# A fused attention and state-space kernel: small VectorE work moved to GpSimd, table chains reordered, 86 quads in place of 84

## The chip, the core and the metric

The kernel runs on one core of a Trainium2 chip. The metric is the device time of one execution in microseconds (us); less is better. The core has five engines with a queue each: TensorE (PE, matrix products; its weight loads are listed as PEld), ScalarE (ACT), VectorE (DVE), GpSimd (POOL) and SyncE (SP), which issues nearly all DMAs.

## The reference

The input is one sequence of 2048 positions and 512 features. Cut to what matters:

```python
g = sigmoid((x * gate_w).sum(-1, keepdims=True))
# A: softmax attention, 32 heads of 16
q, k, v = split(x @ wqkv)
p = softmax(einsum("bhqd,bhkd->bhqk", q, k) * 16 ** -0.5)
a = merge(einsum("bhqk,bhkd->bhqd", p, v)) @ wo
# B: a state-space convolution over the sequence, per feature d
P = exp(dt * A[:, :, None] * l)             # complex, l = 0 .. 2047
K = einsum("dn,dnl,dn->dl", C, P, dt * B).real
b = causal_conv(x, K) + x * Dskip           # by FFT in the reference
out = g * a + (1 - g) * b
```

## The kernel before

**Attention.** The 32 heads by 2048 keys by 2048 queries are cut into tiles of 128 keys by 512 queries. Four tiles (four heads, one key block) make a q step; there are 512 q steps in 32 blocks of 16, 2048 tiles in all. Tiles are put into 683 groups of three. For a group g, `qk` computes the score tiles into one of two PSUM buffers (SC0, SC1), and `ex` takes the exponential of the group in one ScalarE instruction (line 939) into a ring of tiles ET/EX. `pv` multiplies a finished q step with the values VE into the PSUM bank OA; one column of VE is 1, so that the sum of the softmax comes along. After 16 q steps `norm_a` transposes OA into OT (line 994); for each pair of blocks `norm_b` takes the reciprocal (L1000), a gate factor in the later half (L1003), and the product ON (L1006); `norm_c` transposes ON into OnT (L1011).

**Quads.** To spare ScalarE, some q steps are done by VectorE: `decide` inserts the four tiles of such a step, one per group, as third tiles of four groups, and ScalarE then runs over two tiles only. VectorE evicts each of the four score tiles with one multiply-add into 16-bit integers, which read as bf16 are a rough exponential (`bits`, tile DZ, L960). `batch` adds three constants (CUTS) to the whole quad, giving three more versions, DU (L974, 2048 integers per partition each), and `sums` adds all four versions up through value products on TensorE. `win` decides whether a quad may start: it needs a window of groups (WIN, from group 190 to 674), a distance from the last quad, and a count of quads under a line with slope 1 per RATE groups; `decide` also wants idle VectorE time in the plan.

**State-space part.** `params` builds powers of the complex decay (L1 to L80, M1 to M9) by squaring and complex products on VectorE, `powers`, `weights` and `zpart` build the tables B16 and Z for each quarter of the features (`tables` for the first, `bases` for the others, which go through DRAM), and for each of 16 blocks of features a table T is multiplied out. `kstage` makes the taps with matrix products into the PSUM bank MB, transposes them into Kt (L1311), and copies rows of them with shifts into Ks (L1315 and L1318), which goes to DRAM (gm_kd). From there come the Toeplitz tiles H, and `ystage` computes the convolution with the rows U (from `xrows`) into MB, gated into Yst (L1406).

**Order.** The program is not written out by hand: generators (`norms`, `projs`, `tables` and the others) yield pieces of work with an engine, a cost and a priority, and a planner (`Sched.fill`) puts them between the groups by its own model of each engine's time, in which each operation has a cost `c`. The queues are then fixed, in the planned order, with semaphore waits; `place` gives the tiles their SBUF addresses. The function `zero` issues products with a zero tile wm between the useful ones, with amounts FILL. Paced DMAs wait for a marker (`tk`) that the exponential of an earlier group sets.

Of the kernel before, what the change touches and what calls it, by code (L numbers as in the profile page):

```python
# [39 lines left out]
SPLAG = .8  # L40
PTM = 3.2
# [11 lines left out]
RATE = 5.9  # L53
RATE2 = 5.4
# [72 lines left out]
class Prog:  # L127
# [68 lines left out]
    def ready(self, a):  # L196
        eng, R, W = a[1][0], a[1][2], a[1][3]
        lag = SPLAG if a[0] == self.dma else .05
        t = 0.0
        for acc, wr in ((R, False), (W, True)):  # L200
            for b, sl, *tag in acc:
                st = b.st.get(sl)
                if not wr and (st is None or not st[0] or (tag and b.tags.get(sl) != tag[0])):
                    return None
                if st is None:
                    continue
                for d in (st[0], st[1]) if wr else (st[0],):
                    for s, i in d.items():
                        if s != "PE" or eng != "PE":
                            t = max(t, self.fin[(s, i)] + (.03 if s == eng else self.marg.get((s, i), DMARG) if isinstance(s, tuple) else DLAG if eng == 'PE' and s == 'DVE' else lag))  # L210
        return t
# [65 lines left out]
    def dma(self, eng, fn, R=(), W=(), c=.45, lat=3.0, m=DMARG, pace=False, b=.1):  # L277
# [12 lines left out]
        at = self.tm[eng]  # L290
        for s2, k2 in deps.items():
            at = max(at, self.fin[(s2, k2)] + (.08 if isinstance(s2, tuple) else SPLAG))
# [195 lines left out]
def declare(nc, es):  # L488
# [56 lines left out]
    for n in ("WW", "WN", "L1", "L2", "L4", "L8", "L16", "L32", "L64", "L80", "M1", "M2", "M4", "M8", "M9", "pt1", "pt2"):  # L545
        sb(n, 2 * D, FP32)
# [120 lines left out]
def dap(t, off, dims):  # L667
    return bass.AP(tensor=t, offset=off, ap=[list(d) for d in dims])

# [5 lines left out]
def record(nc, p, B, ins):  # L675
# [290 lines left out]
    def batch(i):  # L966
# [5 lines left out]
        for n, (u, cut) in enumerate(zip(us, CUTS)):  # L972
            yield ("DVE", .6)
            op("DVE", lambda v, u=u, cut=cut: v.tensor_scalar(u.u16(0, [[1, 2048]]), z.u16(0, [[1, 2048]]), float(cut), None, ALU.add),  # L974
               R, [(u, 0, i)], c=.07 + 2048 / 3840)
            sch.mark(f"u{i}.{n}")
# [19 lines left out]
    def norm_b(b, n):  # L996
        w = b % 2 + 1 - n
        R = [(OT, x, b - b % 2 + x) for x in range(w, w + n)]
        K = range(w, w + n)
        op("DVE", lambda v: v.reciprocal(Rz(16 * w, [[16, n], [1, 16]]), OT(512 * w + 16, [[512, n], [32, 16]])), R, [(Rz, x) for x in K], c=.22 + .02 * n)  # L1000
        qc = b // 8
        if qc >= 2:
            op("DVE", lambda v: v.tensor_tensor(Rz(16 * w, [[16, n], [4, 4], [1, 4]]), Rz(16 * w, [[16, n], [4, 4], [1, 4]]),  # L1003
                                                B["gq"](4 * (qc - 2), [[0, n], [1, 4], [8, 4]]), ALU.mult),
               [(Rz, x) for x in K] + [(B["gq"], j) for j in range(4)], [(Rz, x) for x in K], c=.12)
        op("DVE", lambda v: v.tensor_tensor(ON(16 * w, [[16, n], [32, 16], [1, 16]]), OT(512 * w, [[512, n], [32, 16], [1, 16]]),  # L1006
                                            Rz(16 * w, [[16, n], [1, 16], [0, 16]]), ALU.mult), R + [(Rz, x) for x in K], [(ON, x) for x in K], c=.07 + .27 * n)

# [19 lines left out]
    def cmul(o, x, y, kind=""):  # L1028

        o, x, y, t1, t2 = B[o], B[x], B[y], B["pt1"], B["pt2"]  # L1030
# [13 lines left out]
    def square(o, x, conj=False):  # L1044
# [5 lines left out]
        tt("DVE", half(o, 0), half(t1, 0), half(t1, 1), ALU.subtract, [(t1, 0)], [(o, 0)], F5)  # L1050
        yield ("DVE", F5)
        op("DVE", lambda v: v.scalar_tensor_tensor(o(D, [[1, D]]), x(0, [[1, D]]), -2.0 if conj else 2.0, x(D, [[1, D]]), ALU.mult, ALU.mult),
           [(x, 0)], [(o, 0)], c=F5)

# [14 lines left out]
    def params():  # L1069
# [7 lines left out]
        for o, x in (("L2", "L1"), ("L4", "L2"), ("L8", "L4")):  # L1077
            yield from square(o, x)
        sch.mark("L8")
        for o, x in (("L16", "L8"), ("L32", "L16"), ("L64", "L32")):  # L1080
            yield from square(o, x)
        yield from square("M1", "L64", True)
# [3 lines left out]
        for o, a, b_, f in seq:  # L1086
# [6 lines left out]
            else:  # L1093
                tt("DVE", full(o), full(a), full(b_), f, key(a, b_), key(o), F5)
        yield from cmul("WN", "WW", "M1")
        for o, x in (("M2", "M1"), ("M4", "M2")):
            yield from square(o, x)
        sch.mark("M4")
        yield from square("M8", "M4")
        yield from cmul("M9", "M8", "L32", "xc")  # L1100
        yield from short("M8", "")
        yield from short("L32", "c")
        yield from short("M9", "")
        yield from cmul("L80", "L64", "L16")
        for n in ("L16", "L64", "L80"):
            yield from short(n, "n")

    def weights(qr, last, top):

        FP, t1, t2 = B["FP"], B["ft1"], B["ft2"]  # L1110
        d0 = 128 * qr
        e8 = 128 * 8
        for l, n in enumerate(("WW", "WN")):
            yield ("DVE", .38)
            op("DVE", lambda v, l=l, n=n: v.tensor_copy(FP(128 * l, [[e8, 2], [1, 128]]), B[n](d0, [[D, 2], [1, 128]])), key(n), [(FP, 0)], c=.25)
        for m, ln in ((2, "M2"), (4, "M4")):
            L, ts = B[ln], 128 * m
            yield ("LOCK", "FT")
            for ti, ri in ((t1, 0), (t2, 1)):
                yield ("DVE", dv(2 * ts))  # L1120
                tt("DVE", lambda ti=ti, ts=ts, m=m: ti(0, [[ts, 2], [128, m], [1, 128]]), lambda m=m: FP(0, [[e8, 2], [128, m], [1, 128]]),
                   lambda ri=ri, m=m, L=L: L(ri * D + d0, [[0, 2], [0, m], [1, 128]]), ALU.mult,
                   [(FP, 0), (L, 0)], [(ti, 0)], dv(2 * ts))
            for part, f in ((0, ALU.subtract), (1, ALU.add)):
                yield ("DVE", dv(ts))
                tt("DVE", lambda part=part, m=m, ts=ts: FP(part * e8 + 128 * m, [[1, ts]]), lambda part=part, ts=ts: t1(part * ts, [[1, ts]]),
                   lambda part=part, ts=ts: t2((1 - part) * ts, [[1, ts]]), f, [(t1, 0), (t2, 0)], [(FP, 0)], dv(ts))
            sch.unlock("FT")
        yield ("DVE", 1.2)
        op("DVE", lambda v: v.tensor_copy(last(0, [[last.free // 2, 2], [1, 1024]]), FP(0, [[e8, 2], [1, 1024]])), [(FP, 0)], top, c=1.2)  # L1130

    def powers(qr, last, top, *tag):

        FP, t1, t2 = B["FP"], B["ft1"], B["ft2"]
        d0, e8, l8 = 128 * qr, 128 * 8, last.free // 2

        def row(k, n=1, step=1):
            return lambda: FP(128 * k, [[e8, 2], [128 * step, n], [1, 128]])

        def rows(part, k, n=1, step=1):  # L1140
            return FP(part * e8 + 128 * k, [[128 * step, n], [1, 128]])
# [4 lines left out]
        def times(k, n, step, ln, out, W, chop=False):  # L1146
            L, ts = B[ln], 128 * n
            yield ("LOCK", "FT")
            for ti, ri in ((t1, 0), (t2, 1)):
                yield ("DVE", dv(2 * ts))  # L1150
                tt("DVE", lambda ti=ti: ti(0, [[ts, 2], [128, n], [1, 128]]), row(k, n, step),
                   lambda ri=ri: L(ri * D + d0, [[0, 2], [0, n], [1, 128]]), ALU.mult, [(FP, 0), (L, 0)], [(ti, 0)], dv(2 * ts))
            pat = [[128, n], [32, 4], [1, 32]] if chop else [[128, n], [1, 128]]
            for part, f in ((0, ALU.subtract), (1, ALU.add)):
                yield ("DVE", dv(ts))
                tt("DVE", lambda part=part: out(part), lambda part=part: t1(part * ts, pat), lambda part=part: t2((1 - part) * ts, pat), f,
                   [(t1, 0), (t2, 0)], W, dv(ts))
            sch.unlock("FT")

        def squares(k, n, out, W, chop=False):  # L1160
            ts = 128 * n
            one = [[32, 4], [1, 32]] if chop else [[1, 128]]
            pat = [[128, n]] + one
            yield ("LOCK", "FT")
            yield ("DVE", dv(2 * ts))
            tt("DVE", lambda: t1(0, [[ts, 2], [128, n], [1, 128]]), row(k, n), row(k, n), ALU.mult, [(FP, 0)], [(t1, 0)], dv(2 * ts))
            yield ("DVE", dv(ts))
            for j in range(n):
                op("DVE", lambda v, j=j: v.scalar_tensor_tensor(out(1, j, 1), FP(128 * (k + j), one), 2.0, FP(e8 + 128 * (k + j), one), ALU.mult, ALU.mult),
                   [(FP, 0)], W, c=dv(128))  # L1170
            yield ("DVE", dv(ts))
            tt("DVE", lambda: out(0), lambda: t1(0, pat if n > 1 else one), lambda: t1(ts, pat if n > 1 else one), ALU.subtract, [(t1, 0)], W, dv(ts))
            sch.unlock("FT")

        yield ("DVE", .2)
        op("DVE", lambda v: v.memset(FP(0, [[1, 128]]), 1.0), [], [(FP, 0)], c=.1)
        op("DVE", lambda v: v.memset(FP(e8, [[1, 128]]), 0.0), [], [(FP, 0)], c=.1)
        for k, n in ((1, "L1"), (2, "L2"), (4, "L4")):
            yield ("DVE", .25)
            op("DVE", lambda v, k=k, n=n: v.tensor_copy(FP(128 * k, [[e8, 2], [1, 128]]), B[n](d0, [[D, 2], [1, 128]])), key(n), [(FP, 0)], c=.22)  # L1180
        yield from times(1, 1, 1, "L2", lambda part: rows(part, 3), [(FP, 0)])
        yield from times(1, 2, 2, "L4", lambda part: rows(part, 5, 2, 2), [(FP, 0)])
        yield from squares(3, 1, lambda part, j=0, n=1: FP(part * e8 + 768, [[1, 128]]), [(FP, 0)])
# [586 lines left out]
```

## Time and profile before

| | |
|---|---|
| median of 3 runs | 801.1 us (800.99 to 801.3) |
| profiled execution | 801.08 us, span 799.3 us |
| busy in the span | PE 697.3, ACT 783.4, DVE 732.7, POOL 10.2 us |
| granted TensorE clock | 0.999 of full speed |
| DMA | 95.37 MB, mean 119 GB/s |

Times in rows of the profile are us from the start of the span, and durations in us unless called ns. A row of a group reads: line, engine, operation, output <- input, shapes, count | busy us, mean ns | idle time of the engine ahead of these instructions, and who ended it. In a row of the timeline or of the chain the first two numbers are start and length; square brackets hold idle time before it. In the stage rows the first range is the stretch, then its length, then the busy time (and instructions) of PE, PEld, DVE, ACT and POOL, the granted clock, the DMA share and GB/s. Rows of the same engine overlap at their edges: an instruction's record begins before the one ahead of it has drained.

### The profile page before, as it was taken

The numbers are of one execution on the slowest core, as the hardware profiler recorded it, in microseconds if no ns is written. First come the engines' busy times: TensorE is split into PE (matmuls) and PEld (weight loads), VectorE is DVE, ScalarE is ACT, GpSimd is POOL, SyncE is SP. The second block draws the span as 40 slices with busy tenths as digits, with TensorE's granted clock in tenths as the row PEclk, the third lists the DMA queues.
The fourth block names the chain that finished last, engine by engine and source line by source line (L and its number), as shares of the span: only waits on it lengthen the run. The fifth ranks groups of instructions, "written<-read, shape, count | busy, mean of one in ns | idle before, by whom it ended". The sixth has DMA issues, their size and how long they took to land.

```text
span 799.3 us, 29251 instructions
## 1 busy us (share of the span) xinstructions
PE 697.3 (87%) x13073; PEld 289.6 (36%) x13073; DVE 732.7 (92%) x1249; ACT 783.4 (98%) x694; POOL 10.2 (1%) x16
## 2 busy tenths in 40 slices
PE   7888888887787888989999888999989999889996
PEld 3222333432244333444434343334434444322221
DVE  7999998999999899999998999989998979899993
ACT  7999999999999999999999999999999999999995
POOL 5000000000000000000000000000000000000000
PEclk9999999999999999999999999999999999999999
DMA  9443001134365666634544555555564556531100
GB/s 211 94 89 79 9 9 37 36 103 142 111 184 149 195 168 167 177 102 132 147 106 140 173 159 161 159 132 141 144 163 121 163 149 162 134 85 53 37 22 28
DMA packets 138640, 95.37 MB, mean 119 GB/s; under 512 B 86033, under 2 KB 117138, under 8 KB 138130
## 3 DMA queue, kind: packets, MB, share of 16 engines
q1 hardware_dynamic: 136498, 92.32, 43.4%
q8 instruction: 102, 1.67, 0.9%
q10 hardware_dynamic: 2016, 1.18, 0.6%
q14 instruction: 24, 0.20, 0.1%
HBM read 65.38 MB, written 19.42 MB: 106 GB/s over the span
## 4 chain that ended last, share of the span: by engine, by line
ACT 94%; PE 3%; DVE 1%; DMA 1%; issue 0%; ACTq 0%; DVEq 0%
ACT ET L939 78%; ACT EX L939 16%; PE SC L690 1%; DMA Wk<-in_A_wqkv_dram 1%; PE MB L690 1%; PE OA L690 0%; DVE DZ L960 0%; ACTq L694 0%; DVE OT L994 0%; DVE B16s L1130 0%; DVEq L652 0%; DVE KT L780 0%; DVE ON L1006 0%; ACT ea L1073 0%; DVE fo L1731 0%
## 5 line engine op out<-in xcount | busy, mean ns | idle before, releaser
L939 ACT ACTIVATE ET<-SC 128x1536 bf16<-128x1536 f32 (+1 forms) x555 | 656.8, 1535 | 2.9 <-PE OA L690 1.7
L690 PE MATMUL SC<-Qm,KT 32*128 32x512 bf16 x2048 | 273.7, 384 | 84.3 <-ACT ET L939 65.1
L960 DVE TENSOR_SCALAR DZ<-SC 128x512 uint16<-128x512 f32 x336 | 224.1, 682 | 21.2 <-PE SC L690 19.8
L690 PEld LDWEIGHTS SC<-Qm,KT 32*128 32x128 bf16 x2048 | 70.3, 91 | 287.8 <-ACT ET L939 213.1
L974 DVE TENSOR_SCALAR DU<-DZ 128x2048 uint16<-128x2048 uint16 x252 | 165.1, 686 | 0.7
L690 PE MATMUL OA<-wm 128*32 128x256 bf16 (+3 forms) x962 | 163.5, 341 | 1.2 <-DVE wm L743 1.2
L690 PE MATMUL OA<-ET,VE 128*32 128x512 bf16 x1420 | 153.3, 389 | 1.2 <-DVE OT L994 0.9
L939 ACT ACTIVATE EX<-SC 128x1024 bf16<-128x1024 f32 (+1 forms) x128 | 147.1, 1350 | 0.0
L690 PE MATMUL OA<-DU,VE 128*32 128x512 bf16 x1008 | 96.2, 385 | 0.0
L690 PEld LDWEIGHTS MB<-U,H 128*32 128x32 bf16 x4096 | 82.0, 144 | 25.8 <-issue 16.4
L690 PE MATMUL MB<-U,H 128*32 128x128 bf16 (+7 forms) x4096 | 88.7, 225 | 1.2 <-issue 1.0
L690 PEld LDWEIGHTS OA<-ET,VE 128*32 128x32 bf16 x1420 | 39.4, 94 | 70.1 <-issue 65.6
L1015 DVE TENSOR_TENSOR T<-B,DT 128x1536 bf16<-128x1536 bf16 x64 | 59.0, 946 | 0.0
L690 PEld LDWEIGHTS OA<-wm 128*32 128x32 bf16 (+2 forms) x962 | 43.4, 94 | 16.3 <-issue 13.5
L690 PEld LDWEIGHTS MB<-T,Z 128*32 128x32 bf16 x2048 | 43.7, 155 | 10.5 <-issue 6.5
L690 PE MATMUL MB<-T,Z 128*32 128x64 bf16 (+1 forms) x2048 | 45.7, 235 | 0.2 <-issue 0.2
L690 PE MATMUL OA<-EX,VE 128*32 128x512 bf16 x292 | 40.4, 387 | 0.3 <-ACT ET L939 0.3
L690 PEld LDWEIGHTS OA<-DU,VE 128*32 128x32 bf16 x1008 | 25.7, 96 | 30.7 <-issue 21.1
L690 PE MATMUL OA<-DZ,VE 128*32 128x512 bf16 x336 | 33.0, 383 | 0.0
L994 DVE STREAM_TRANSPOSE OT<-OA 128x512 f32<-128x512 f32 x32 | 22.9, 715 | 8.9 <-PE OA L690 8.7
L1406 DVE TENSOR_TENSOR Yst<-MB,gt 128x512 bf16<-128x512 f32 x32 | 21.9, 684 | 2.0 <-PE MB L690 2.0
L1015 DVE TENSOR_TENSOR ft<-Z,DM 128x1024 bf16<-128x1024 bf16 x32 | 20.9, 686 | 0.3
(144 smaller groups left out, 445.1 us busy)
## 6 DMA issues: line engine op xcount, KB each, us to landing
H<-gm_kd SPq DMA_DIRECT2D x128, 256.0 KB, 3.6
U<-gm_xs SPq DMA_DIRECT2D x128, 134.2 KB, 2.7
T<-B SPq DMA_DIRECT2D x16, 256.0 KB, 2.6
gm_yd<-Yst SPq DMA_DIRECT2D x64, 64.0 KB, 2.7
gm_bd<-B16s SPq DMA_DIRECT2D x3, 1024.0 KB, 5.6
B<-gm_bd SPq DMA_DIRECT2D x12, 256.0 KB, 3.1
gm_kd<-Ks SPq DMA_DIRECT2D x64, 40.0 KB, 2.1
gm_xs<-xP SPq DMA_DIRECT2D x16, 136.0 KB, 2.5
```

Source lines behind the costliest of these rows:

```text
L690: op("PE", lambda t: t.matmul(out(), lhsT(), rhs(), start=start, stop=stop, skip_group_check=True, **kw), R, W, c=c, lat=.15, a=a, cfg=cfg)
L939: op("ACT", lambda a: a.activation(E(at, [[1, 512 * n]]), sc(0, [[1, 512 * n]]), AF.Exp, scale=DH ** -0.5), [(sc, i, g) for i in range(n)] ...
L960: op("DVE", lambda v: v.tensor_scalar(z.u16(512 * k, [[1, 512]]), sc(1024, [[1, 512]]), XS, XB, ALU.mult, ALU.add), [(sc, 2, g)], [(z, k, ...
L974: op("DVE", lambda v, u=u, cut=cut: v.tensor_scalar(u.u16(0, [[1, 2048]]), z.u16(0, [[1, 2048]]), float(cut), None, ALU.add), R, [(u, 0, i ...
L994: op("DVE", lambda v: v.transpose(OT(512 * w, [[1, 512]]), OA(0, [[1, 512]])), [(OA, 0, b)], [(OT, w, b)], c=.64)
L1015: op(eng, lambda v: v.tensor_tensor(o(), a(), b_(), f), R, W, c=c)
L1406: op("DVE", lambda v, w=w, h=h: v.tensor_tensor(Yst(1024 * w + 4 * h, [[128, R8], [8, 16], [1, 4]]), MB(0, [[1, R8], [R8, 16], [NC, 4]]), ...
```

## The change

- GpSimd gets the tap row copies into Ks (`kstage`), the first of the three additions of every sixth quad (numbers 3, 9, 15 and so on), one in four of the paired norm products (`norm_b` with b = 3, 11, 19, 27), and the fills of xP and gt.
- Quads may come closer (RATE 5.3 in place of 5.9 and 5.4) but only while enough tap blocks are done (`done`), which gives 86 of them by the words of the change.
- `params` is split into two threads; in it, in `weights`, `powers` and `zpart` the operations are reordered so that an operation and the one that reads its result are separated by another, with finer keys for the halves of the scratch tiles and a third scratch tile pt3. `weights` writes its last half directly into its target.
- The planner's lag for the marker of paced DMAs is 0.15 in place of 0.8 us.

```diff
+TLAG = .15
-RATE = 5.9
+RATE = 5.3
+KA = 6.5
+PKS = "POOL"
+PGS, PGR, PGN, PGM = 6, 3, 4, 1
+KB = 46
-RATE2 = 5.4
+RATE2 = 5.3
...
-                            t = max(t, self.fin[(s, i)] + (.03 if s == eng else ...
+                            t = max(t, self.fin[(s, i)] + (TLAG if b.name == "tk" else .03 if s == eng else ...
...
+def pl(n):
+    return .3 + n / 600
...
+    def done():
+        return next((k for k in range(NBLK) if f"K{k}" not in sch.flag), 99)
+
     def win(x):
         return next((w for w, (lo, hi, _, gap, *_) in enumerate(WIN) if lo <= x < hi and x >= plan["x"] + gap
-                     and len(sets) <= (min(x, XR) - WIN[0][0]) / RATE + max(x - XR, 0) / RATE2), None)
+                     and len(sets) <= (min(x, XR) - WIN[0][0]) / RATE + max(x - XR, 0) / RATE2 and done() >= KA + (x - WIN[0][0]) / KB), None)
...
         for n, (u, cut) in enumerate(zip(us, CUTS)):
-            yield ("DVE", .6)
-            op("DVE", lambda v, u=u, cut=cut: v.tensor_scalar(u.u16(0, [[1, 2048]]), z.u16(0, [[1, 2048]]), float(cut), None, ALU.add),
-               R, [(u, 0, i)], c=.07 + 2048 / 3840)
+            eng = "POOL" if n == 0 and i % PGS == PGR else "DVE"
+            yield (eng, .6)
+            op(eng, lambda v, u=u, cut=cut: v.tensor_scalar(u.u16(0, [[1, 2048]]), z.u16(0, [[1, 2048]]), float(cut), None, ALU.add),
+               R, [(u, 0, i)], c=pl(2048) if eng == "POOL" else .07 + 2048 / 3840)
...
-        op("DVE", lambda v: v.tensor_tensor(ON(...), OT(...), Rz(...), ALU.mult), ..., c=.07 + .27 * n)
+        eng = "POOL" if n == 2 and b // 2 % PGN == PGM else "DVE"
+        yield (eng, .6, 1)
+        op(eng, lambda v: v.tensor_tensor(ON(...), OT(...), Rz(...), ALU.mult), ..., c=pl(256 * n) if eng == "POOL" else .07 + .27 * n)
...
+        yield from square("M1", "L64", True)
+        sch.mark("M1")
+        for o, x in (("M2", "M1"), ("M4", "M2"), ("M8", "M4")):
+            yield from square(o, x)
+            sch.mark(o)
+
+    def params2():
+        yield ("AFTER", "L2")
...
     def zpart(qr):
...
-                for ti, xr, yr in ((t1, 0, part), (t2, 1, 1 - part)):
...
+        yield from mul(0, 0)
+        yield from mul(0, 1)
+        for u in range(1, 6):
+            yield from mul(u, 0)
+            yield from add(u - 1)
+            yield from mul(u, 1)
+        yield from add(5)
...
-        yield ("DVE", .65)
+        yield (PKS, .65)
         for q in range(2):
-            op("DVE", lambda v, q=q: v.tensor_copy(Ks(5 * HW * q + HW, ...
+            op(PKS, lambda v, q=q: v.tensor_copy(Ks(5 * HW * q + HW, ...
...
-            op("DVE", lambda v, k=k: v.memset(xP(k * T * XW, [[XW, T], [1, 16]]), 0.0), [], [(xP, (0, k))], c=.45)
+            op("POOL", lambda v, k=k: v.memset(xP(k * T * XW, [[XW, T], [1, 16]]), 0.0), [], [(xP, (0, k))], c=.45)
...
-        op("DVE", lambda v: v.memset(B["gt"](0, [[1, NC]]), 0.0), [], [(B["gt"], j) for j in range(8)], c=.2)
+        op("POOL", lambda v: v.memset(B["gt"](0, [[1, NC]]), 0.0), [], [(B["gt"], j) for j in range(8)], c=.3)
```

More of the change, by code (lines that the diff above doesn't have):

```diff
@@ L209, in ready @@
                         if s != "PE" or eng != "PE":
[L210 removed]
+                            t = max(t, self.fin[(s, i)] + (TLAG if b.name == "tk" else .03 if s == eng else self.marg.get((s, i), DMARG) if isinstance(s, tuple) else DLAG if eng == 'PE' and s == 'DVE' else lag))
         return t
@@ L1100, in params @@
+        yield ("AFTER", "M8")
         yield from cmul("M9", "M8", "L32", "xc")
         yield from short("M8", "")
-        yield from short("L32", "c")
         yield from short("M9", "")
-        yield from cmul("L80", "L64", "L16")
-        for n in ("L16", "L64", "L80"):
-            yield from short(n, "n")
-    def weights(qr, last, top):
-        FP, t1, t2 = B["FP"], B["ft1"], B["ft2"]
-        d0 = 128 * qr
-        e8 = 128 * 8
-        for l, n in enumerate(("WW", "WN")):
[L1114 to L1130, printed above, removed]
@@ L1132, in powers @@
     def powers(qr, last, top, *tag):
-        FP, t1, t2 = B["FP"], B["ft1"], B["ft2"]
+        FP = B["FP"]
         d0, e8, l8 = 128 * qr, 128 * 8, last.free // 2
[L1137 to L1141, printed above, removed]
+        rw = lambda *k: [(FP, x) for x in k]
+        one, cut = [[1, 128]], [[32, 4], [1, 32]]
+        hi, lo = [(last, (1, 4), *tag)], [(last, (1, 0), *tag)]
@@ L1167, in squares, with add @@
+        def add(part, h, n, out, W, pat):
+            ts = 128 * n
             yield ("DVE", dv(ts))
-            for j in range(n):
-                op("DVE", lambda v, j=j: v.scalar_tensor_tensor(out(1, j, 1), FP(128 * (k + j), one), 2.0, FP(e8 + 128 * (k + j), one), ALU.mult, ALU.mult),
-                   [(FP, 0)], W, c=dv(128))
-            yield ("DVE", dv(ts))
-            tt("DVE", lambda: out(0), lambda: t1(0, pat if n > 1 else one), lambda: t1(ts, pat if n > 1 else one), ALU.subtract, [(t1, 0)], W, dv(ts))
@@ L1173, in squares @@
[L1173 to L1181, printed above, removed]
@@ L1182, in powers @@
-        yield from times(1, 2, 2, "L4", lambda part: rows(part, 5, 2, 2), [(FP, 0)])
-        yield from squares(3, 1, lambda part, j=0, n=1: FP(part * e8 + 768, [[1, 128]]), [(FP, 0)])
-        yield from times(1, 4, 2, "L8", lambda part: place(part, 9, 4), [(last, (1, 4), *tag)], True)
-        yield ("DVE", .4)
-        op("DVE", lambda v: v.tensor_copy(last(256, [[l8, 2], [512, 4], [2, 32]]), B["L8"](d0, [[D, 2], [32, 4], [1, 32]])), key("L8"), [(last, (1, 0), *tag)], c=.34)
-        yield from squares(5, 3, lambda part, j=0, n=3: place(part, 10 + 2 * j, n), [(last, (1, 0), *tag)], True)
+            tt("DVE", lambda: out(part), lambda: ft(0, h, part * ts, pat), lambda: ft(1, h, (1 - part) * ts, pat),
+               ALU.add if part else ALU.subtract, ftk(0, h) + ftk(1, h), W, dv(ts))
@@ new lines, in diff, with low @@
+        def diff(h, n, out, W, pat):
+            ts = 128 * n
+            yield ("DVE", dv(ts))
+            tt("DVE", lambda: out(0), lambda: ft(0, h, 0, pat), lambda: ft(0, h, ts, pat), ALU.subtract, ftk(0, h), W, dv(ts))
+        def low(part, h):
+            yield ("DVE", .55)
+            op("DVE", lambda v: v.tensor_copy(place(part, h, 4), FP(part * e8 + 128 * h, [[256, 4], [32, 4], [1, 32]])),
+               rw(*range(h, 8, 2)), [top[part]], c=.42)
+        yield ("LOCK", "FT")
+        yield from copy(1, "L1")
@@ new lines, in powers @@
+        yield from mul(0, 0, 1, 1, "L2")
+        yield from mul(1, 0, 1, 1, "L2")
+        yield from copy(2, "L2")
+        yield from add(0, 0, 1, lambda part: FP(part * e8 + 384, one), rw(3), one)
+        yield from add(1, 0, 1, lambda part: FP(part * e8 + 384, one), rw(3), one)
+        yield from copy(4, "L4")
+        yield from mul(0, 1, 1, 2, "L4")
+        yield from mul(1, 1, 1, 2, "L4")
+        yield from sqr(0, 3, 1)
+        for part in range(2):
+            yield from add(part, 1, 2, lambda part: FP(part * e8 + 640, [[256, 2], [1, 128]]), rw(5, 7), [[128, 2], [1, 128]])
@@ new lines, in powers @@
+        yield from diff(0, 1, lambda part: FP(part * e8 + 768, one), rw(6), one)
+        yield from cross(3, lambda part: FP(part * e8 + 768, one), rw(6), one)
+        yield ("DVE", .4)
+        op("DVE", lambda v: v.memset(FP(0, one), 1.0), [], rw(0), c=.1)
+        op("DVE", lambda v: v.memset(FP(e8, one), 0.0), [], rw(0), c=.1)
+        op("DVE", lambda v: v.tensor_copy(last(256, [[l8, 2], [512, 4], [2, 32]]), B["L8"](d0, [[D, 2], [32, 4], [1, 32]])), key("L8"), lo, c=.34)
+        yield from sqr(2, 5, 3)
@@ L1719, in record @@
     norm_a(31)
-    norm_b(31, 1)
+    for _ in norm_b(31, 1):
+        pass
     norm_c(31)
```

180 lines of the change are left out of this document (116 added, 64 removed).

## The prediction

> **What bounds the kernel now.** I read the page's busy line first, then the chain that ended last, then ScalarE's waits, and only then VectorE, from which most of the moved work is taken.
>
> ```profile
> PE 697.3 (87%) x13073; PEld 289.6 (36%) x13073; DVE 732.7 (92%) x1249; ACT 783.4 (98%) x694; POOL 10.2 (1%) x16
> ACT 94%; PE 3%; DVE 1%; DMA 1%; issue 0%; ACTq 0%; DVEq 0%
> 84.32 180.05 ACT ET L939 x134
> 787.64 1.35 ACT ET L939
> 794.03 0.82 DVEq L652
> ```
>
> ScalarE (ACT) is busy 98% of the 799.3 us span and makes 94% of the chain. It runs the 683 exponentials, one behind another, until 788.99; about 10.3 us of last products and stores follow. The 134 exponentials from 84.32 to 264.37 are all three tiles wide and follow one another without a gap, so one takes 180.05 / 134 = 1.344 us of ScalarE.
>
> ```profile
> L939 ACT ACTIVATE ET<-SC 128x1024 bf16<-128x1024 f32 x240 | 245.4, 1208 | 1.9 <-PE OA L690 1.7 <-PE SC L690 0.2
> L939 ACT ACTIVATE ET<-SC 128x1536 bf16<-128x1536 f32 x117 | 178.4, 1629 | 0.5 <-PE SC L690 0.4
> L939 ACT ACTIVATE EX<-SC 128x1024 bf16<-128x1024 f32 x92 | 97.7, 1227 | 0.0
> L939 ACT ACTIVATE EX<-SC 128x1536 bf16<-128x1536 f32 x35 | 55.5, 1661 | 0.0
> ```
>
> These are the groups of the window 274.31 to 785. The mean durations (1.2 and 1.6 us) overlap their neighbours and must not be summed; the spacing is what counts. The window has 510.7 us, less 2.4 us of idle time in these rows: 508.3 us for 332 two-wide and 152 three-wide exponentials. With 152 x 1.344 = 204.3 for the wide ones, a two-wide one takes 304.0 / 332 = 0.916 us. **A tile taken off ScalarE is therefore worth 1.344 - 0.916 = 0.428 us**, provided that ScalarE keeps going without gaps. So far it does:
>
> ```profile
> ACT fo L1733 <- PE SC L690: 3.9, 1, 3.9
> ACT ET L939 <- PE OA L690: 1.7, 1, 1.7
> ACT ET L939 <- PE SC L690: 1.0, 4, 0.4
> PE SC L690 <- ACT ET L939: 71.1, 194, 0.9
> PE SC L690 <- DVE DZ L960: 0.9, 3, 0.4
> ```
>
> The exponentials wait 2.7 us in all; TensorE waits for ScalarE 194 times, hardly ever for VectorE. The score tiles are always there in time. The limit is how many tiles ScalarE must take, and that is set by how many quads VectorE takes instead.
>
> **Part 1: two more quads.** A quad is four tiles whose exponentials VectorE builds from bits. There are 336 DZ evictions, so 84 quads; 86 are announced. Two quads take 8 tiles from ScalarE: 8 x 0.428 = **3.4 us off the path**. The number of exponentials stays at 683, eight of them turn from three tiles wide to two. TensorE gains nothing and pays 2 x 12 more value products (three added tiles for each tile of a quad); its DU products, 1008 in 96.2 us of overlapping records, are covered by the 71.1 us in which TensorE waits for ScalarE.
>
> ```profile
> L690 PE MATMUL OA<-DU,VE 128*32 128x512 bf16 x1008 | 96.2, 385 | 0.0
> L960 DVE TENSOR_SCALAR DZ<-SC 128x512 uint16<-128x512 f32 x336 | 224.1, 682 | 21.2 <-PE SC L690 19.8
> L974 DVE TENSOR_SCALAR DU<-DZ 128x2048 uint16<-128x2048 uint16 x252 | 165.1, 686 | 0.7
> ```
>
> A quad costs VectorE 4 x 0.682 + 3 x 0.686 = 4.8 us, so two cost 9.6 us.
>
> **Part 2: what leaves VectorE.**
>
> ```profile
> L1315 DVE CAST Ks<-Kt 128x256 bf16<-128x256 f32 x32 | 7.8, 284 | 0.0
> L1318 DVE CAST Ks<-Kt 128x56 bf16<-128x56 f32 (+1 forms) x32 | 4.6, 187 | 0.0
> L1006 DVE TENSOR_TENSOR ON<-OT,Rz 128x512 bf16<-128x512 f32 (+1 forms) x17 | 11.2, 661 | 0.6
> 280.00:680.00 400.00, 364.73 (x8101) 167.14 (x8097) 376.12 (x630) 397.87 (x378) 0.00 (x0) 1.00 0.55 148
> 680.00:785.00 105.00, 96.16 (x1319) 28.54 (x1311) 97.87 (x161) 105.00 (x103) 0.00 (x0) 1.00 0.24 63
> ```
>
> Gone are the 64 tap row copies (7.8 + 4.6 = 12.4 us), the first additions of quads 3, 9, ... 81 (14 x 0.686 = 9.6 us), and 4 of the paired norm products (about 4 x 0.69 = 2.8 us); the pad and gate memsets are under 1 us. That is 24.8 us off VectorE against 9.6 us added: 15 us net. The two stage rows show (third busy figure) VectorE 376 of 400 and 98 of 105 us busy, so 31 us were free there already. VectorE isn't the chain; this room is worth nothing by itself. It pays only through the two quads.
>
> **Part 3: the chains.** Table building is reordered so that an operation no longer stands right behind the one that it reads.
>
> ```profile
> 113.09 1.29 DVE L1015 TENSOR_TENSOR ft<-Z,DL 128x1024 bf16<-128x1024 bf16 x2
> 114.42 0.69 DVE L1015 TENSOR_TENSOR Z<-ft,ft 128x1024 bf16<-128x1024 bf16 x1
> ```
>
> Two independent products occupy 1.29 us with 0.69 us each, so the second starts 0.60 us after the first; the sum that reads them starts 0.73 us after the second. A broken dependence saves some 0.13 us of VectorE. With at most about 200 such places that is at most 26 us, nearly all ahead of the quads, where ScalarE has no gap to give back: priced at zero. What covers it is ScalarE itself, gapless from 84.32 to 264.37. The lower bound of this part and of the new pacing is the 2.7 us of exponential waits that a better order could remove.
>
> **Part 4: GpSimd as a worker.** The trace has no arithmetic on GpSimd between two SBUF tiles, only fills:
>
> ```profile
> L760 POOL MEMSET VE<- 128x2240 bf16 x4 | 7.7, 1967 | 0.3 <-DVE piota L748 0.3
> L1282 POOL MEMSET Ks<- 128x640 bf16 x2 | 1.2, 636 | 0.0
> ```
>
> The two give (1967 - 636) / 1600 = 0.83 ns an element and 0.1 us fixed. From below, an addition over 2048 elements is then 1.8 us; from above I take what the changed planner reserves, 0.3 + 2048 / 600 = 3.7 us. I take the middle, 2.8 us: reading and adding must cost something over a fill. In the same way a tap row copy of 256 lies between 0.3 and 0.7 us, a norm product of 512 between 0.5 and 1.2 us. GpSimd's total is about 14 x 2.8 + 64 x 0.4 + 4 x 0.9 = 68 us of 799, so it isn't a bound. Who waits: the value products of that addition on TensorE, with all that is queued there behind; the gm_kd writes on SP's queue behind the copies, with the H and U loads behind them; VectorE's transposition into OnT behind the norm product. The writes have cover, since no wait of TensorE or ScalarE after the start ends on a DMA; the transposition can hold VectorE by up to 1.2 us, four times. The planner knows all these waits and places consumers by its 3.7 us. New lag constants for paced loads only move DMA issues by fractions of a microsecond, at a DMA share of 0.55 in the stage row: zero. Without that cover each late addition costs what the rivals price.
>
> **The sum.** Profiled run 801.08 us, span 799.3, so 1.8 us lie outside it; the median of the runs is 801.1, the same. 801.1 - 3.4 = **797.7 us**. About 0.2% (1.6 us) is what a measurement of this kernel can tell from no change.
>
> **Rival A, slower: GpSimd holds VectorE up.** While GpSimd reads SBUF, VectorE instructions that read SBUF as well, the DU additions and the two-input products above all, might have to stand still until it is done. The trace can price such a stop, since it has stops of that kind made by other work:
>
> ```profile
> 270.64 1.22 DVE L1130 CAST B16s<-FP 128x2048 bf16<-128x2048 f32 x1
> 271.77 0.71 DVE L994 STREAM_TRANSPOSE OT<-OA 128x512 f32<-128x512 f32 x1
> 272.40 1.84 DVE L960 TENSOR_SCALAR DZ<-SC 128x512 uint16<-128x512 f32 x3
> 273.11 0.38 PE L690 MATMUL SC<-Qm,KT 32*128 32x512 bf16 x1 [0.44 <-DVE DZ L960]
> 274.31 2.37 ACT L939 ACTIVATE ET<-SC 128x1536 bf16<-128x1536 f32 x2 [0.26 <-PE SC L690]
> ```
>
> Here a DZ eviction stood behind 1.76 us of other VectorE work (270.64 to 272.40); the score tile was freed late, TensorE lost 0.44 and ScalarE 0.26 us. So about 1.5 us of a stop are free and the rest comes through. In the quad stages every second or third VectorE instruction is a DU addition or a table product of the sort in question, the two other additions of the same quad among them, so a stop begins some 0.6 us after GpSimd. An addition of length D costs D - 0.6 - 1.5: nothing at 1.8 us, 0.7 us at 2.8, 1.6 us at 3.7. Times 14: 0, 10 or 22 us, so 798, **808** or 820 us; it turns the sign at D = 2.1 + 3.4 / 14 = 2.35 us. Against it:
>
> ```profile
> 2.28 7.68 POOL L760 MEMSET VE<- 128x2240 bf16 x4 [0.32 <-DVE piota L748]
> 7.31 0.68 DVE L1015 TENSOR_TENSOR bn<-AimT,dt 128x512 f32<-128x512 bf16 x1
> 8.03 0.69 DVE L1621 SCALAR_TENSOR_TENSOR ba<-bn 128x512 f32<-128x512 f32 x1
> ```
>
> These two-input operations ran inside GpSimd's VE fills (2.28 to 9.96) at their usual length, but a fill only writes, so this speaks to half of the question. The Trainium skill, page SBUF — State Buffer, section Who interferes with whom, states this very lock: a VectorE instruction with two SBUF inputs, or in a mode that uses both of its ports, and a GpSimd instruction that reads SBUF exclude each other, and whoever is second stands still for the other's whole length. By that rule rival A would hold wherever D is over 2.35 us; no run so far shows it. Chance 0.20.
>
> **Rival B, slower or even: a late addition holds TensorE.** If D is above the reserved 3.7 us, the value products wait, and score products behind them.
>
> ```profile
> 345.34 0.40 PE L690 MATMUL OA<-ET,VE 128*32 128x512 bf16 x4 [0.87 <-DVE OT L994]
> 345.77 5.54 ACT L939 ACTIVATE ET<-SC 128x1024 bf16<-128x1024 f32 x5 [1.70 <-PE OA L690]
> ```
>
> That 0.87 us wait of TensorE cost ScalarE 1.70 us. An addition of 4.2 us, 0.5 late, would by this ratio cost about 1 us, 14 us in all: 812 us. The fills, twice as fast as reserved, speak against it. Chance 0.06.
>
> **Rival C, no change:** the quads come, but the new order opens about 14 ScalarE gaps of some 0.2 us, the size of those that exist (1.0 us in 4), 3 us in all: 800.7 us. That fewer than 86 quads appear belongs here too (84 would give 801.1). Chance 0.08.
>
> **How the numbers follow.** The forecast has 0.66, its own range 795.0 (3.4 and all 2.7 us of waits gone) to 799.4. Rivals A and B together have 0.26 and lie above 802.7. The range goes from 795.0 to 808, the middle of rival A, which leaves out about half of A and B and little else. Faster 0.66, same 0.08, slower 0.26.
>
> **What would show it.** Right: 344 DZ evictions, 345 two-wide exponentials (337 before) at the same spacing, ScalarE waits still near 3 us, DU on VectorE 244 times and on POOL 14 times at 2 to 3.5 us, VectorE busy near 718 us. Wrong: VectorE records of 2 us and more beside POOL's (rival A), "PE OA waits for POOL" rows (B), ScalarE idle time beyond 6 us, or a tail after the last exponential clearly over 10.3 us.

## The result: 9% slower, and the profile after

The changed kernel takes 874.8 us (874.33 to 875.41, 4 runs) against 801.2 us, a ratio of 1.0916 with a 95% interval of 1.0902 to 1.0931. The forecast was 797.7 us. The profiled execution has a span of 873.6 us. The busy line and the chain of the changed kernel, to be set beside those of before:

```profile
PE 730.0 (84%) x13053; PEld 294.1 (34%) x13053; DVE 777.2 (89%) x1188; ACT 785.5 (90%) x694; POOL 134.7 (15%) x103
ACT 63%; PE 19%; DVE 13%; issue 4%; DMA 1%; ACTq 0%; DVEq 0%
```

ScalarE was 94% of the chain and is now 63%: the rest of the chain runs mostly through TensorE and VectorE, while ScalarE waits (it is busy for 90% of the span; it was 98%). VectorE, which was to lose 15 us of work, is busy for 777 us in place of 733. The groups on the additions and on GpSimd's other work, and ScalarE's and TensorE's waits, say how that comes (group rows: busy us, mean ns, idle time before; wait rows: us in total, times, longest):

```profile
L973 DVE TENSOR_SCALAR DZ<-SC 128x512 uint16<-128x512 f32 x344 | 228.7, 681 | 29.1 <-PE SC L700 27.5
L988 DVE TENSOR_SCALAR DU<-DZ 128x2048 uint16<-128x2048 uint16 x244 | 224.3, 944 | 0.8
L988 POOL TENSOR_SCALAR DU<-DZ 128x2048 uint16<-128x2048 uint16 x14 | 80.1, 5718 | 289.6 <-DVE DZ L973 258.2 <-PE MB L700 31.4
L1399 POOL CAST Ks<-Kt 128x256 bf16<-128x256 f32 x32 | 24.7, 799 | 286.6 <-DVE Kt L1395 286.4
L1024 POOL TENSOR_TENSOR ON<-OT,Rz 128x512 bf16<-128x512 f32 x4 | 4.9, 1230 | 62.4 <-DVE Rz L1019 42.6 <-DVE Rz L1016 19.8
...
ACT ET L952 <- PE SC L700: 63.1, 38, 5.4
ACT EX L952 <- PE SC L700: 10.7, 6, 4.8
...
PE SC L700 <- DVE DZ L973: 36.1, 15, 4.2
PE OA L700 <- POOL DU L988: 5.0, 3, 1.9
```

The 344 DZ evictions are 86 quads, as announced. A GpSimd addition takes 5.72 us, not 2.8 (the planner had reserved 3.7). The additions left on VectorE take 944 ns on the mean in place of 686, 63 us more in all. The exponentials wait 73.8 us for score tiles; before, their waits were 2.7 us in all. One of the 14 events in VectorE's, GpSimd's and TensorE's timeline (start, length):

```profile
291.65 5.74 POOL L988 TENSOR_SCALAR DU<-DZ 128x2048 uint16<-128x2048 uint16 x1 [16.82 <-DVE DZ L973]
292.07 5.85 DVE L988 TENSOR_SCALAR DU<-DZ 128x2048 uint16<-128x2048 uint16 x1
297.85 0.67 DVE L973 TENSOR_SCALAR DZ<-SC 128x512 uint16<-128x512 f32 x1
298.58 0.60 PE L700 MATMUL SC<-Qm,KT 32*128 32x512 bf16 x1 [4.03 <-DVE DZ L973]
300.70 1.02 ACT L952 ACTIVATE ET<-SC 128x1024 bf16<-128x1024 f32 x1 [4.85 <-PE SC L700]
```

The next VectorE instruction, another addition that takes 0.69 us by itself, begins 0.42 us after GpSimd's and ends at 297.92, half a microsecond after GpSimd's has ended (297.39). A DZ eviction stands behind it, its score tile is freed late, TensorE idles 4.03 us and ScalarE 4.85. Each of the 14 additions has such a held VectorE record beside it. Thirteen times it is a DU addition of 3.28 to 5.85 us that ends about half a microsecond after GpSimd's; once it is a table product of two SBUF tiles, of 4.28 us where 0.95 is usual, and that one ends (397.49) before GpSimd's does (398.42):

```profile
393.05 5.37 POOL L988 TENSOR_SCALAR DU<-DZ 128x2048 uint16<-128x2048 uint16 x1
393.21 4.28 DVE L1033 TENSOR_TENSOR T<-B,DT 128x1536 bf16<-128x1536 bf16 x1
```

The stages of the first event (length; PE, PEld, DVE, ACT, POOL busy; granted clock) show a second loss behind the first:

```profile
291.65:294.50 2.85, 2.85 (x100) 1.82 (x89) 2.85 (x2) 2.85 (x4) 2.85 (x1) 1.00 0.72 191
294.50:298.58 4.08, 0.05 (x3) 0.01 (x1) 4.08 (x3) 1.34 (x2) 2.88 (x1) 0.74 0.62 186
298.58:303.84 5.26, 5.26 (x66) 1.60 (x66) 4.38 (x8) 2.76 (x3) 0.00 (x0) 0.56 0.15 40
303.84:306.00 2.16, 2.14 (x31) 0.54 (x28) 2.16 (x4) 2.11 (x3) 0.00 (x0) 1.00 0.67 164
```

While TensorE idles its granted clock falls (0.74 on the mean of that stretch), and it stays near half for 5.26 us after the work has come back: score products take 0.60 us in place of 0.39 just when they are needed most. Behind each of the 14 additions there is a stretch at a granted clock of 0.50; their sum over the run is:

```profile
sum 95.58, PE 79.54 PEld 20.27 DVE 79.83 ACT 46.19 POOL 8.15; mean PE 5.68 PEld 1.45 DVE 5.70 ACT 3.30 POOL 0.58
```

### The profile page after: what moved, and what is told of

Its sections match the earlier page's. It is cut to its first block, busy times and chain, and to the rows that moved or that the text cites. A ratio compares the mean times of both kernels' runs of the same rounds, so it can differ in the third digit from the quotient of the medians.

```text
span 873.6 us, 29283 instructions
## 1 busy us (share of the span) xinstructions
PE 730.0 (84%) x13053; PEld 294.1 (34%) x13053; DVE 777.2 (89%) x1188; ACT 785.5 (90%) x694; POOL 134.7 (15%) x103
## 4 chain that ended last, share of the span: by engine, by line
ACT 63%; PE 19%; DVE 13%; issue 4%; DMA 1%; ACTq 0%; DVEq 0%
ACT ET L952 54%; ACT EX L952 9%; PE OA L700 8%; PE SC L700 8%; DVE DU L988 6%; DVE DZ L973 4%; PE MB L700 3%; DVE T L1033 1%; DMA Wk<-in_A_wqkv_dram 1%; DVE Kt L1395 0%; DVE OT L1008 0%; DVE Yst L1490 0%; DVE fo L1614 0%; DVE ft L1033 0%; DVE OnT L1029 0%
## 5 line engine op out<-in xcount | busy, mean ns | idle before, releaser
L952 ACT ACTIVATE ET<-SC 128x1024 bf16<-128x1024 f32 (+1 forms) x556 | 655.8, 1505 | 64.5 <-PE SC L700 63.1
L700 PE MATMUL SC<-Qm,KT 32*128 32x512 bf16 x2048 | 290.0, 400 | 111.2 <-ACT ET L952 57.6
L988 DVE TENSOR_SCALAR DU<-DZ 128x2048 uint16<-128x2048 uint16 x244 | 224.3, 944 | 0.8
L988 POOL TENSOR_SCALAR DU<-DZ 128x2048 uint16<-128x2048 uint16 x14 | 80.1, 5718 | 289.6 <-DVE DZ L973 258.2
L700 PE MATMUL OA<-DU,VE 128*32 128x512 bf16 x1032 | 105.5, 421 | 5.1 <-POOL DU L988 5.0
L700 PE MATMUL MB<-U,H 128*32 128x88 bf16 (+7 forms) x4096 | 89.7, 228 | 0.8 <-issue 0.8
L1399 POOL CAST Ks<-Kt 128x256 bf16<-128x256 f32 x32 | 24.7, 799 | 286.6 <-DVE Kt L1395 286.4
L1033 DVE TENSOR_TENSOR T<-B,DT 128x1536 bf16<-128x1536 bf16 x64 | 64.4, 1038 | 0.0
L700 PE MATMUL MB<-T,Z 128*32 128x48 bf16 (+1 forms) x2048 | 46.8, 235 | 0.2 <-issue 0.2
L1395 DVE STREAM_TRANSPOSE Kt<-MB 128x512 f32<-128x512 f32 x16 | 11.3, 704 | 31.1 <-PE MB L700 31.1
```

Of the source, the lines that this page charges most:

```text
L700: op("PE", lambda t: t.matmul(out(), lhsT(), rhs(), start=start, stop=stop, skip_group_check=True, **kw), R, W, c=c, lat=.15, a=a, cfg=cfg)
L952: op("ACT", lambda a: a.activation(E(at, [[1, 512 * n]]), sc(0, [[1, 512 * n]]), AF.Exp, scale=DH ** -0.5), [(sc, i, g) for i in range(n)] ...
L988: op(eng, lambda v, u=u, cut=cut: v.tensor_scalar(u.u16(0, [[1, 2048]]), z.u16(0, [[1, 2048]]), float(cut), None, ALU.add), R, [(u, 0, i)] ...
L1033: op(eng, lambda v: v.tensor_tensor(o(), a(), b_(), f), R, W, c=c)
L1395: op("DVE", lambda v: v.transpose(Kt(0, [[1, 512]]), MB(0, [[1, 512]])), ky, [(Kt, 0, blk)], c=.66)
L1399: op(PKS, lambda v, q=q: v.tensor_copy(Ks(5 * HW * q + HW, [[8, 4], [HW // 2, 8], [1, 8]]), Kt(256 * q, [[64, 4], [8, 8], [1, 8]])), [(Kt, ...
```

## Experiments

Three theories stood against one another: **hold** (rival A: VectorE stands still while GpSimd adds), **late result** (rival B: TensorE waits for an addition that was planned at 3.7 us) and **order** (the rewritten chains, pacing and admission are bad by themselves).

**The additions alone put back.** The recorded plan is replayed with the engine of the 14 additions changed; queue order and addresses stay.

```diff
+            if f.__name__ == "op" and a[0] == "POOL" and (a[3][0][0].name.startswith("DU")):
+                a = ("DVE",) + a[1:]
             (prog.op if f.__name__ == "op" else prog.dma)(*a)
```

> The changed kernel with its plan and queue order as they are; only the 14 first additions run on VectorE, at the place where the plan has them. Lock theory (VectorE stands still for the whole of each 5.7 us GpSimd addition, ScalarE loses about 5 us each time): nearly all of the 77 us goes, 797 to 803 us, the DU records of VectorE back at 0.69 us, granted clock back at 0.99 or more. Late-result theory (TensorE waits for an addition that takes 5.7 us where 3.7 us were planned): also back to about 800 us, so this run doesn't tell the two apart. Order theory (the rewritten chains, the pacing or the admission made a bad order): still above 860 us.

Measured 799.17 us against 801.49, ratio 0.9976 (0.9964 to 0.9988). The whole loss, 75.6 us, hangs on 14 instructions; the order theory is out; the other two both expected this.

```profile
ACT ET L954 <- PE SC L702: 1.4, 6, 0.3
```

**The additions alone moved, in the kernel before.** It is planned anew with them, at the same 3.7 us each.

```diff
-            yield ("DVE", .6)
-            op("DVE", lambda v, u=u, cut=cut: v.tensor_scalar(u.u16(0, [[1, 2048]]), ...
+            eng = "POOL" if n == 0 and i % 6 == 3 else "DVE"
+            yield (eng, .6)
+            op(eng, lambda v, u=u, cut=cut: v.tensor_scalar(u.u16(0, [[1, 2048]]), ...
```

> The kernel before, planned anew with the first addition of every sixth quad on GpSimd at the planner's 3.7 us, and nothing else of the change: 84 quads, 14 additions moved. Lock theory: 14 x 5.5 us = 77 us more than before, 865 to 885 us. Order theory: within 5 us of before, 796 to 806 us.

Measured 873.24 us, ratio 1.0905 (1.0874 to 1.0936). Nearly the same loss (71.8 us) without any other part of the change.

**The additions cut into four.** At replay, each is issued as four of 512 elements.

```diff
+                for k in range(4):
+                    prog.op("POOL", lambda v, u=u, z=z, k=k: v.tensor_scalar(u.u16(512 * k, [[1, 512]]), z.u16(512 * k, [[1, 512]]), float(CUTS[0]), None, ALU.add), a[2], a[3])
+                continue
```

> The changed kernel with plan and order as they are; each of the 14 GpSimd additions is cut into four of 512 elements that wait for one another. Lock theory, with the lock held for one instruction: a piece of about 1.4 us holds VectorE for at most that long, about the 1.5 us that were free in the kernel before, so most of the loss goes: 805 to 830 us, no VectorE record above 2.2 us, granted clock above 0.98. Late-result theory: the last piece is done as late as before or later, so 865 us or more. Order theory: about 875 us.

Measured 862.15 us, ratio 1.0767 (1.0745 to 1.0789): a miss for the hold theory alone. The groups and TensorE's waits of this run show that the hold is nearly gone and that the late result has taken its place:

```profile
L993 DVE TENSOR_SCALAR DU<-DZ 128x2048 uint16<-128x2048 uint16 x244 | 170.0, 721 | 5.6 <-PE OA L705 4.8
L672 POOL TENSOR_SCALAR DU<-DZ 128x512 uint16<-128x512 uint16 x56 | 97.5, 1742 | 278.6 <-DVE DZ L978 246.0 <-PE MB L705 29.1
...
PE OA L705 <- POOL DU L672: 42.2, 14, 4.1
PE SC L705 <- DVE DZ L978: 1.6, 4, 0.8
```

VectorE's additions are back at 721 ns, and TensorE now waits 14 times for GpSimd, 42.2 us, where it waited 36.1 us for VectorE. Four pieces take 7.0 us, 3.3 more than the plan has; the value products stand in TensorE's queue at the planned place, with the next score products behind them. In the changed kernel the two waits lay on top of each other, so that little of the second was seen (the 5.0 us above).

**Both removed, and one.** Planned anew with the true length of the additions (7.6 us in place of `pl(2048)`), and cut; planned anew with 5.9 us, and whole.

```diff
-               R, [(u, 0, i)], c=pl(2048) if eng == "POOL" else .07 + 2048 / 3840)
+               R, [(u, 0, i)], c=7.6 if eng == "POOL" else .07 + 2048 / 3840)    # 5.9 for the whole ones
```

> The changed kernel planned anew with 7.6 us in place of 3.7 for a GpSimd addition, and each addition cut into four pieces, so that the consumers on TensorE stand where the result really is there: 87 quads. Two-mechanism theory (the hold of VectorE and the late result for TensorE each cost some 4 us of TensorE idle time plus a clock drop, and either alone is enough): with both gone 801.1 - 12 x 0.43 = 796 us, 794 to 802, clock 0.99. Lock-only theory, where cutting should have been enough and something else keeps split4 slow: still above 850 us.

> The changed kernel planned anew with 5.9 us in place of 3.7 for a GpSimd addition, the additions whole: 89 quads, 15 additions on GpSimd. Late result gone, hold of VectorE left. Two-mechanism theory: 801.1 - 20 x 0.43 + 15 x about 5 = 865 us (845 to 880), VectorE records of 5.8 us. Late-result theory: 793 to 798 us.

Cut and planned: 812.15 us, ratio 1.0134 (1.0116 to 1.0152). Whole and planned: 884.71 us, ratio 1.1052 (1.1028 to 1.1075), with VectorE records of 5.86 us, and 5 us above the expected range. The new plans have 87 and 89 quads, so they differ from the changed kernel in more than the additions. Still, each of the two is enough alone: the late result of the cut additions costs 63 us (862.15 - 799.17), and the hold of the whole ones about 92 us against the 792.5 us that 89 quads would give. With both treated, 50 us of the first come back. The 812 missed the expected 794 to 802: ScalarE still waits 16.0 us. Its waits, and one of TensorE's that was 0.9 us, once, in the kernel before:

```profile
ACT ET L957 <- PE OA L705: 8.0, 7, 2.6
ACT EX L957 <- PE SC L705: 4.3, 7, 1.5
ACT ET L957 <- PE SC L705: 3.7, 6, 1.0
PE OA L705 <- DVE OT L1013: 3.0, 6, 1.0
```

Half of that is waiting for value products, in five of the seven cases right behind a wait of TensorE for VectorE's transposition into OT. The pieces still hold VectorE's additions, but only to about 1.1 us (1.27 us at most). Whether these short holds or the new plan make the rest late is open; no run isolates it.

**The length of the addition.** With plan and order as they are, GpSimd adds only the first half, or the first quarter, of the tile.

```diff
+                prog.op("POOL", lambda v, u=u, z=z: v.tensor_scalar(u.u16(0, [[1, 1024]]), z.u16(0, [[1, 1024]]), float(CUTS[0]), None, ALU.add), a[2], a[3])
```

> The changed kernel with plan and order as they are; each GpSimd addition covers the first 1024 of 2048 elements and the other half of that sum is left out of the computation. The addition should take 2.8 to 2.9 us, less than the 3.7 us planned, so the result is in time and only the hold of VectorE is left, at the length that the prediction had assumed. The prediction's formula (D - 2.1 us each, 14 times): 797.7 + 11 = 809 us, 803 to 815. A formula with no free part (D each): 838 us. No hold at all: 798 us.

> The changed kernel with plan and order as they are; each GpSimd addition covers the first 512 of 2048 elements, the rest of that sum is left out of the computation. The addition should take 1.5 us. If holds of up to about 2.1 us after all are free, as the prediction's formula has it (nothing below D = 2.1): 799 us, as adds_back, 797.5 to 801. If each hold costs in proportion to its length (806.0 - 799.2 over 3.2 us, times 1.6): 802.6 us.

Half: 806.01 us, ratio 1.0057 (1.0041 to 1.0074). Quarter: 797.28 us, ratio 0.9951 (0.9936 to 0.9965). Their rows in GpSimd's and VectorE's groups, half first:

```profile
L671 POOL TENSOR_SCALAR DU<-DZ 128x1024 uint16<-128x1024 uint16 x14 | 44.8, 3203 | 274.3 <-DVE DZ L977 244.4 <-PE MB L704 29.7
L992 DVE TENSOR_SCALAR DU<-DZ 128x2048 uint16<-128x2048 uint16 x244 | 174.0, 737 | 0.8
ACT ET L956 <- PE SC L704: 9.0, 15, 1.2
```

```profile
L992 DVE TENSOR_SCALAR DU<-DZ 128x2048 uint16<-128x2048 uint16 x244 | 167.4, 711 | 0.8
L671 POOL TENSOR_SCALAR DU<-DZ 128x512 uint16<-128x512 uint16 x14 | 28.8, 2059 | 281.2 <-DVE DZ L977 250.7 <-PE MB L704 30.4
ACT ET L956 <- PE SC L704: 0.9, 2, 0.6
```

With the additions back on VectorE as zero, the price goes: none at 2.06 us, 6.8 us at 3.20, 75.6 at 5.72. Short holds are free, as the prediction had it (the quarters came out just under their range of 797.5 to 801), and beyond that the price climbs faster than the length. Two things climb with it. VectorE's own additions grow by 6, 12 and 63 us in all (711, 737 and 944 ns in place of 686), which is 0.4, 0.9 and 4.5 us for each GpSimd addition: the hold itself isn't in proportion to the length. And the granted clock is 1.00 with quarters, 0.993 with halves and 0.945 whole. How the price divides between the two no run shows.

**Fills in place of additions.** Two fills of the tile, which read nothing; the kernel leaves the first of the quad's three added versions out.

```diff
+                for k in range(2):
+                    prog.op("POOL", lambda v, u=u: v.memset(u(0, [[1, 2048]]), 0.0), a[2], a[3])
+                continue
```

> The changed kernel with plan and order as they are; in place of each GpSimd addition stand two fills of the same tile, 3.7 us together, that read nothing (the sum's first version is left out). If a GpSimd instruction that only writes holds VectorE's DU additions too, some DU records are 1.2 to 2.5 us long, and the time stays at 797 to 803 us, since 1.8 us at a time is within what is free; if only reading holds them, all DU records are below 1 us. Time in both cases about that of adds_back, 797 to 803 us.

Measured 828.77 us, ratio 1.0349 (1.0334 to 1.0365): the kind of hold came as the first case had it, the time was a miss by 26 us. The group of VectorE's additions, and the event at the same place:

```profile
L993 DVE TENSOR_SCALAR DU<-DZ 128x2048 uint16<-128x2048 uint16 x244 | 191.9, 811 | 0.8
291.62 4.09 POOL L672 MEMSET DU<- 128x2048 bf16 x2 [16.64 <-DVE DZ L978]
292.07 1.90 DVE L993 TENSOR_SCALAR DU<-DZ 128x2048 uint16<-128x2048 uint16 x1
293.89 0.67 DVE L978 TENSOR_SCALAR DZ<-SC 128x512 uint16<-128x512 f32 x1
294.49 1.77 DVE L993 TENSOR_SCALAR DU<-DZ 128x2048 uint16<-128x2048 uint16 x1
```

Here each fill holds one addition, to 1.90 and 1.77 us. Two holds with one eviction between them add up (1.2 + 1.1 us of VectorE), so the slack seems to be there once for the two, not once for each; the granted clock fell too, to 0.974.

**The smaller moves.** All of GpSimd's additions, copies and products back, planned anew (85 quads); then, at replay, additions and norm products back, and additions and tap copies back; last, only the tap copies on GpSimd, planned anew with KA = 6 (87 quads).

```diff
-PKS = "POOL"
-PGS, PGR, PGN, PGM = 6, 3, 4, 1
+PKS = "DVE"
+PGS, PGR, PGN, PGM = 6, 9, 4, 9
...
+            if f.__name__ == "op" and a[0] == "POOL" and (a[3][0][0].name == "ON" or a[3][0][0].name.startswith("DU")):
+                a = ("DVE",) + a[1:]
...
+            if f.__name__ == "op" and a[0] == "POOL" and (a[3][0][0].name.startswith("DU") or a[3][0][0].name.startswith("Ks") and a[3][0][1] != "z"):
+                a = ("DVE",) + a[1:]
...
-KA = 6.5
+KA = 6
```

> The changed kernel, planned anew, with the additions, the tap row copies and the norm products all on VectorE; chains, pacing and admission stay changed. The planner then places 85 quads, one less than with GpSimd and one more than before. Lock theory: 801.1 - 4 x 0.43 = 799.4 us, 797.5 to 802. Order theory: above 850 us.

> The changed kernel with plan and order as they are; the first additions and the four norm products on VectorE, only the tap row copies on GpSimd. If the norm products on GpSimd (1.23 us each) hold VectorE and delay its transposition noticeably: 797 to 798.5 us, below adds_back; if they are free: 798.5 to 800.

> The changed kernel with plan and order as they are; the first additions and the tap row copies on VectorE, only the norm products on GpSimd. VectorE gets 12 us of short copies in places where the plan has none. If VectorE's room counts now: 801 to 804 us, near all_back; if it doesn't: 799 to 800.

> The changed kernel planned anew with additions and norm products on VectorE, tap row copies on GpSimd, and KA at 6 in place of 6.5: 87 quads. 12 tiles fewer on ScalarE than before: 801.1 - 5.1 = 796.0 us if nothing else is lost; with the loss that adds_back shows against its own sum (1.5 us) 797.5 us. Range 795.5 to 801; above 801 VectorE has become the limit, as all_back's 803.4 with 85 quads would have it.

All back: 803.40 us, ratio 1.0026 (1.0013 to 1.0039), above its range of 797.5 to 802. Additions and norm products back: **798.24 us, ratio 0.9964 (0.9952 to 0.9976)**, 0.4% below the kernel before and the best complete version here. Additions and taps back: 801.52, ratio 1.0003 (0.9993 to 1.0013). Taps only with 87 quads: 800.54, ratio 0.9994 (0.9982 to 1.0005). ScalarE's waits, in the order of the last three:

```profile
ACT ET L954 <- PE SC L702: 0.8, 4, 0.2
```

```profile
ACT ET L954 <- PE SC L702: 4.1, 10, 1.2
```

```profile
ACT ET L952 <- PE SC L700: 5.1, 8, 1.3
```

The tap copies on GpSimd are worth 2.4 us (801.52 - 799.17, both with the norm products on GpSimd) with 86 quads: without the room on VectorE that they make, the gain of the quads goes into late score tiles (4.1 us of waits against 1.4). The norm products on GpSimd cost 0.9 us (799.17 - 798.24), which the intervals don't separate from nothing; with them there an addition of VectorE at 341.76 is held to 1.55 us beside a norm product of 1.38 us. The plan with an 87th quad is 2.3 us slower than 798.24; whether the quad or the new plan does that isn't shown.

## Why the prediction was wrong

- **What bounds the kernel, and 0.43 us for a tile: held.** 86 quads without GpSimd additions are 2.3 us (adds_back) to 3.0 us (norm products back too) faster than before; 3.4 were forecast. The run with 797.28 us leaves out most of a sum and shows only that nothing else was lost.
- **The step that failed is the overlap, in part 4 and the sum.** The sum puts the 14 GpSimd additions at nothing, as if VectorE worked on beside them, and leaves the hold to rival A. The runs show VectorE's additions held, 63 us of them in all, and a price of 75.6 us. The length isn't what turned the sign: by the text's own rule (it turns at 2.35 us) the 2.8 us that it took would already have cost 10 us, and the half additions, at 3.20 us the run nearest to that, cost 6.8 us, twice what the quads were to bring.
- **The length D of a GpSimd addition, in part 4, was mis-sized as well, and made the loss large.** The ends were 1.8 us (a fill's rate) and 3.7 us (the planner's own cost), the middle was taken. It is 5.72 us. The three sizes give (5.36 - 1.49) / 1536 = 2.5 ns an element from the shortest records of whole and quarter, three times a fill's 0.83. The planner's cost isn't a measurement and was no upper end. The same estimate was low for the smaller moves too: a copy of 256 takes 0.80 us where 0.7 was the upper end, and a product of 512 takes 1.23 where it was 1.2.
- **Rival A, at 0.20, was the right mechanism.** Its rule for the price, D - 2.1 us each, gives 15 us for halves (3.2 us), measured 6.8; and 51 us for whole ones, measured 75.6. Too dear for short holds, too cheap for long ones. It lacked two things. The hold isn't D - 0.6 (2.6 and 5.1 us): VectorE's additions grew by 0.9 us for each half and 4.5 us for each whole one. And the clock falls: in the 14 stretches at 0.50 TensorE worked 79.5 us, about 40 us more than at full clock. How much of these 40 us lies on the path isn't shown, since no run holds the clock up through a stall.
- **Rival B, at 0.06, was true too and hidden behind A.** The prediction called it a late addition above 3.7 us; 5.7 is. In the changed kernel its sign was there, three waits of 5.0 us in all; only the cut additions showed it in full, with 42.2 us.
- **"This room is worth nothing by itself" (part 2) was wrong by 2.4 us**, as adds_taps_back against adds_back shows. VectorE at 94% of the quad stages was no chain, but it had no further 12 us of small copies to give at the places where they fell.
- **Part 3 and the pacing at zero:** nothing contradicts it, but all_back, at 803.4 with 85 quads, loses 4.0 us against its sum with 6.0 us of exponential waits. Whether the new order or the fuller VectorE does that is open.
- **The range** ended at 808 because rival A was cut off at the assumed middle length; its own upper end, 820, was also too low.

The Trainium skill, page SBUF — State Buffer, section Who interferes with whom, states the hold; the runs agree with it: an addition of 5.74 us held a 0.69 us VectorE addition to 5.85 us, one of 5.37 us held a two-input product of 0.95 us to 4.28, and a fill held the additions (1.90 us) but not, in the start of the kernel before, the two-input operations (0.68 and 0.69 us). They differ in one thing: a hold was not always for the whole of the other instruction. The product just named ended 0.9 us before GpSimd's addition, and with the half additions the first held VectorE addition ended at 293.02 and GpSimd's only at 294.21. The measurement decides; why it is so wasn't tried. It goes with VectorE's small loss beside the halves (0.9 us each).

```profile
291.07 3.14 POOL L671 TENSOR_SCALAR DU<-DZ 128x1024 uint16<-128x1024 uint16 x1 [16.17 <-DVE DZ L977]
291.49 1.53 DVE L992 TENSOR_SCALAR DU<-DZ 128x2048 uint16<-128x2048 uint16 x1
293.55 1.22 DVE L992 TENSOR_SCALAR DU<-DZ 128x2048 uint16<-128x2048 uint16 x1
```

## What to carry to other kernels

An idle engine isn't free room if its work makes a busy engine stand still: price the move by the longest instruction it adds, against the slack of what is queued behind the held one, and measure that length before planning with it. Where two waits start from one cause, removing one only uncovers the other. Treating both here brought 50 of 63 us back and still left the kernel at 812 us, above the 801 us of the kernel before. Keep such side work in instructions shorter than the slack (here 2.06 us cost nothing and 3.20 us did), and expect a stall of the matrix engine to cost its clock as well.

## What the runs showed of the hardware

- A 16-bit integer addition on GpSimd takes 5.7 us for 2048 elements, 3.2 us for 1024 and 1.5 us for 512 at best (2.06 on the mean beside VectorE); the same addition takes VectorE 0.69 us. A float copy of 256 elements takes GpSimd 0.8 us, a two-input product of 512 elements 1.23 us against VectorE's 0.69.
- TensorE's granted clock stood at 1.00 for the first 1.86 us of the idle stretch of the first event, at 0.50 for the other 2.16 us, and at 0.50 for 4.67 us of the work behind it. The Trainium skill, page TensorE: Matmul & The Clock Gate, Part 1, puts the fall to half at an idle window of about 3.4 us. The runs don't agree: in this event the clock fell after 1.9 us of idle time, and the fills, with no wait of TensorE for VectorE above 1.8 us, had a granted clock of 0.974 over the run and score products of 0.61 us behind waits of 1.03 and 0.23 us. The measurement decides: shorter gaps were enough.

```profile
294.56:296.42 1.86, 0.00 (x0) 0.00 (x0) 1.86 (x1) 1.28 (x2) 1.86 (x1) 1.00 0.47 143
296.42:298.58 2.16, 0.00 (x1) 0.01 (x1) 2.16 (x3) 0.00 (x0) 0.96 (x1) 0.50 0.74 220
298.58:303.25 4.67, 4.67 (x58) 1.48 (x58) 3.79 (x7) 2.17 (x2) 0.00 (x0) 0.50 0.04 15
```
